# Attention beside a gated MLP mixer on one core: heads prepared in stacks of six, softmax blocks taken two at a time, gelu over two chunks, evacuations first

## The chip, the core and the metric

The kernel runs on one core of a Trainium2 chip. The metric is the time of one execution on the device in microseconds (us). Five engines work in parallel, each through its own queue in order: TensorE (PE, with its weight loads shown as PEld), VectorE (DVE), ScalarE (ACT), GpSimd (POOL) and SyncE (SP), which here only issues DMA transfers.

## The reference

The input x has 2048 tokens of 640 features. The output is x + s * g. Here s is multi-head attention with 32 heads of 20 features, and g is silu of a mixer branch; both start from the layer norm of x.

```python
x = A_x
xn = _layernorm(x)
# A: attention, H = 32, Dh = 20
q, k, v = split(xn @ wqkv)
s = softmax(q k^T * Dh**-0.5) v @ wo
# B: mixer; shift() moves four quarters of the features by +1, -1, +2, -2 tokens
h  = gelu(layernorm(xn) @ w1)
x1 = xn + shift(h) @ w2
b  = x1 + gelu(layernorm(x1) @ w3) @ w4      # w3: 640 x 1536, w4: 1536 x 640
out = x + s * silu(b)
```

## The kernel before

**A program planned by a planner.** The class `Gen` describes the work as tasks: an engine, an estimated duration, what the task reads and writes, and sometimes a due time. `Planner.schedule` carries the due times back through the dependencies to give each task a priority, plays the program forward with its own durations, and so fixes the order of each engine's queue. On the chip the queues then run in that order and wait for each other on semaphores. `strict_engines` names the engines on which a task's class comes before its due time; before, that is PE alone, where the scores and value products (class -1) precede everything else. PSUM banks are handed out by the planner from pools: two double banks for scores (`S`), three single banks (`W`) for everything else that PE computes, and one bank (`PV`) that collects the value products. A task with `rel=h` is the one that empties a bank and gives it back.

**Attention.** The 32 heads go in eight quads of four. For each quad there are four groups of 512 queries, and in each group 16 key tiles of 128 keys. For an ordinary key tile `score_act` computes the scores of two heads into a double bank, and ScalarE takes the exponential of 1024 columns at once (`exp_act`, L1239); `fnpv` (L1186) multiplies by the values and adds into `PV`. A *block* is a pair of key tiles from `BLK` of which half of the heads is taken off ScalarE. `score_both` (scores at L1197) puts two heads into a double bank for ScalarE and the other two into two `W` banks, which VectorE reads into a 16-bit integer buffer `U` (L1270). Four integer operations on `U` (L1160) then make bit patterns whose weighted sum stands for the exponential, and 16 value products (L1175) add the four variants into `PV`. `Cfg.ND` says how many blocks each of the 32 groups has, and `Cfg.order` where they stand among the key tiles. A group ends in `normalise`: VectorE copies `PV` out (L1307), the row sums go through DRAM to be spread over the partitions, inverted (L1314), sent back and broadcast (the DMA of L1318), and multiplied in (L1320). The heads then go to DRAM and from there into `OTd`, the transposed output that stays in SBUF until the end.

**Keys and queries.** `prep(q)` runs once for each quad. It projects the quad's four heads of keys and queries into four groups of 32 partitions (20 used), in 8 tiles of 20 matmuls, each emptied by VectorE (L1048, L1055). It takes the largest key of each feature (L1060), the absolute queries (L1067) and a small product to bound the scores (L1072, L1077), and writes that bound as a 21st row of the queries by four small DMAs (L1079), due `LEAD` = 20 us before the quad's first use. The columns of `wqkv` come in for each quad (L1027).

**The mixer branch.** It runs beside the attention in what PE has left over, with due times spread over the quads (`B1`, `B2`, counted in quads). `b_w12` does one chunk of 512 tokens: w1, a gelu of 2560 columns (L1502), w2 and the residual. `b_w34` does one chunk: layer norm, transposes, w3 with its columns streamed, a gelu of 6144 columns (L1555), w4 from SBUF, the residual (L1564) into `BO`, and the silu through a tanh (L1568) and a product (L1573). The gelu and the exponential are not in one table set, so each gelu brings one table load before it and one after.

**The end.** In the last quad `finish_qc` multiplies by `wo` for each group of 512 queries from `OTd`, multiplies by the gate, adds x and writes the output. `mm_tile` (its matmuls are at L740) is the helper behind every product that isn't attention.

Of the kernel before, what the change touches and what calls it, by code (L numbers as in the profile page):

```python
# [127 lines left out]
class Planner:  # L128
    def __init__(self):
# [16 lines left out]
        self.strict_engines = ("pe",)  # L146
# [124 lines left out]
    def schedule(self, verbose=False):  # L271
# [28 lines left out]
        for t in tasks:  # L300
            if t.cls and t.eng in self.strict_engines:
                t.prio = t.prio + t.cls * self.cls_penalty
# [11 lines left out]
        done = 0  # L314
# [265 lines left out]
class Cfg:  # L580
# [5 lines left out]
    def __init__(self, S=2048, D=640, H=32, F=1536):  # L586
# [13 lines left out]
        self.BLK = [(4, 5), (9, 10), (14, 15)]  # L600
        self.LAG = 3
        self.AHEAD = 3
        self.B1 = (0.4, 0.7)
        self.B2 = (3.0, 1.1)
        self.LEAD = 20000.0
        self.ND = (
            [1, 2, 3, 3],
            [3, 3, 3, 2],
            [3, 3, 3, 2],
            [3, 2, 3, 2],  # L610
            [3, 2, 3, 2],
            [3, 2, 3, 2],
# [3 lines left out]
    def order(self, quad, qc):  # L616

        nb = self.ND[quad][qc]  # L620
        used = [k for b in self.BLK[:nb] for k in b]
        ks = [k for k in range(self.NT) if k not in used]
        at = [round(j * len(ks) / nb) for j in range(nb)]
        out = []
        due = {}
        for i in range(len(ks) + 1):
            for j in range(nb):
                if due.get(j) == i or (i == len(ks) and due.get(j, 0) > i):
                    out.append(("d", j))
                    due[j] = -1  # L630
            for j in range(nb):
                if at[j] == i:
                    out.append(("b", j))
                    due[j] = i + self.LAG
            if i < len(ks):
                out.append(("k", ks[i]))
        return out
# [37 lines left out]
class Gen:  # L675
# [71 lines left out]
    def build(self, plan_only=False):  # L747
        nc, pl = self.nc, self.pl
        with contextlib.ExitStack() as es:
# [5 lines left out]
            self.do = nc.dram_tensor("heads", (2, 128, 512), BF16, kind="Internal").ap()  # L755
            self.W0 = 5
            pl.reserve = 0
# [16 lines left out]
    def program(self):  # L774
# [6 lines left out]
        self.prep_weights(0)  # L781
        self.ln1_and_transpose()
        self.prep(0)
# [4 lines left out]
        for quad in range(cfg.NQUAD):  # L788
            if quad + 1 < cfg.NQUAD:
                self.prep_weights(quad + 1)  # L790
                self.prep(quad + 1)
            if quad == 1:
                self.v_load(1)
                self.v_proj(1)
            self.run_b(quad)
            if quad == cfg.NQUAD - 1:
                self.load_wo()
            self.attn_quad(quad)
# [9 lines left out]
    def setup_consts(self):  # L808
# [26 lines left out]
          reads=[A("maskh")], writes=[A("maskh")], name="maskh")  # L835
        Mm = self.Mm = self.alloc("Mm", [2, 32], BF16)
        T("pool", 200, lambda e: e.memset(Mm[:, :, :], 0.0), writes=[A("Mm", 0), A("Mm", 1)], name="Mm0")

    def alloc_persistent(self):
# [6 lines left out]
        self.AQ = self.alloc("AQ", [S // 2], BF16)  # L846
        self.SH = self.alloc("SH", [512], BF16)
        self.MX = self.alloc("MX", [2], FP32)
        self.Wp = self.alloc("Wp", [2, KC, 92], BF16)
# [3 lines left out]
        self.NSS = 5  # L853
        self.U = self.alloc("U", [2048], U16)
        self.SS = self.alloc("SS", [self.NSS, 2048], U16)
# [5 lines left out]
        self.OTd = self.alloc("OTd", [KC, S], BF16)  # L861
        T("pool", 1500, lambda e: e.memset(self.OTd[:, KC - 1, :], 0.0), writes=[A("OTd", KC - 1, q) for q in range(4)], name="otd0")
# [12 lines left out]
        self.ssi = 0  # L875
# [144 lines left out]
    def prep_weights(self, q):  # L1020
        cfg = self.cfg
        T, A = self.T, self.A
        D, DH = cfg.D, cfg.DH
        src = self.aps["A_wqkv"].rearrange("(kc p) n -> p kc n", p=128)
        for qk in (1, 0):
            c0 = qk * D + q * cfg.QW
            T("sp", C_SP, lambda e, qk=qk, c0=c0: e.dma_start(self.Wp[:, qk, :, :], src[:, :, c0:c0 + 92]),  # L1027
              writes=[A("Wp", qk)], is_dma=True, nbytes=128 * cfg.KC * 92 * 4, name=f"ld_wp{q}_{qk}", stream=f"wp{qk}")

    def prep(self, q):  # L1030

# [4 lines left out]
        b = q % 2  # L1036
# [3 lines left out]
        for qk, dst, tag in ((1, KT, "KT"), (0, QT, "QT")):  # L1040
            for c in range(NQC):
                c0 = 512 * c
                at = [A(tag, b, c)] + ([A("QTa", b, c)] if qk == 0 else [])
                h, wa = self.mm_tile(f"{tag}{q}_{c}", KC, 512, lambda k, j, qk=qk: Wp[:, qk, k, DH * j:DH * j + 32],
                                     lambda k, j, c0=c0: xnT[:, k, c0:c0 + 512],
                                     lambda k, qk=qk, c=c: [A("Wp", qk)] + [A("xnT", k, c)], at)
                if qk == 1:
                    T("dve", c_dve(512), lambda e, h=h, c0=c0: e.tensor_scalar(KT[:, b, c0:c0 + 512], self.wbank(h)[:, 0:512],  # L1048
                                                                               mask[:, 0:1], self.eaug[:, 0:1], op0=ALU.mult, op1=ALU.add),
                      reads=[wa, A("eaug"), A("maskh")], writes=at, name=f"kev{q}_{c}", rel=h)  # L1050
                elif q == 0:
                    T("act", c_act(512) + 100, lambda e, h=h, c0=c0: e.activation(QT[:, b, c0:c0 + 512], self.wbank(h)[:, 0:512], AF.Copy, scale=mask[:, 0:1]),
                      reads=[wa, A("maskh")], writes=at, name=f"qev{q}_{c}", rel=h)
                else:
                    T("dve", c_dve(512), lambda e, h=h, c0=c0: e.tensor_scalar(QT[:, b, c0:c0 + 512], self.wbank(h)[:, 0:512],  # L1055
                                                                               mask[:, 0:1], None, op0=ALU.mult),
                      reads=[wa, A("maskh")], writes=at, name=f"qev{q}_{c}", rel=h)
        MX, Mm, AQ, SH = self.MX, self.Mm, self.AQ, self.SH
        T("dve", c_dve(cfg.S, "1x"),
          lambda e: e.tensor_reduce(MX[:, b:b + 1], KT[:, b, :], axis=AX.X, op=ALU.max, apply_absolute_value=True),  # L1060
          reads=[A("KT", b, c) for c in range(NQC)], writes=[A("MX", b)], name=f"mx{q}")
        T("dve", 210, lambda e: e.tensor_scalar(Mm[:, b, 0:4], self.maskn[:, 0:4], MX[:, b:b + 1], None, op0=ALU.mult),
          reads=[A("MX", b), A("maskn")], writes=[A("Mm", b)], name=f"mm{q}")
        h, wa = self.wtile()
        for k in range(2):
            T("dve", c_dve(cfg.S // 2, "4x"),
              lambda e, k=k: e.tensor_scalar(AQ[:, :].bitcast(U16), QT[:, b, 1024 * k:1024 * k + 1024].bitcast(U16), 0x7FFF, None, op0=ALU.bitwise_and),  # L1067
              reads=[A(t, b, c) for c in (2 * k, 2 * k + 1) for t in ("QT", "QTa")], writes=[A("AQ")], name=f"aq{q}_{k}")
            def fn(e, h=h, k=k):
                pb = self.wbank(h)  # L1070
                for c in (2 * k, 2 * k + 1):
                    ins = e.matmul(pb[32 * c:32 * c + 32, 0:512], Mm[:, b, :], AQ[:, 512 * (c % 2):512 * (c % 2) + 512], start=True, stop=True,  # L1072
                                   tile_position=(0, 32 * c))
                return ins
            T("pe", 216, fn, reads=[A("Mm", b), A("AQ")], writes=[wa] + ([A("SH")] if k == 0 else []), name=f"sh{q}_{k}",
              acq=("W", h) if k == 0 else None, tile=h.id)
        T("dve", c_dve(512), lambda e, h=h: e.tensor_scalar(SH[:, :], self.wbank(h)[:, 0:512], cfg.OFFSET / cfg.scale, None, op0=ALU.add),  # L1077
          reads=[wa], writes=[A("SH")], name=f"shev{q}", rel=h)
        T("sp", 4 * C_SP, lambda e: [e.dma_start(QT[20:128:32, b, 512 * c:512 * c + 512], SH[32 * c:32 * c + 4, :]) for c in range(NQC)],  # L1079
          reads=[A("SH")], writes=[A("QTa", b, c) for c in range(NQC)], is_dma=True, nbytes=16384, name=f"aug{q}", stream="aug", ndma=4,  # L1080
          due=self.due_quad(q) - cfg.LEAD)
# [38 lines left out]
    def attn_quad(self, quad):  # L1120
# [5 lines left out]
        KT, QT, PT, U, SS = self.KT, self.QT, self.PT, self.U, self.SS  # L1126
        VA, VP = self.VA[hf], self.VP[hf]
        PVB = self.PVB
        last = quad == cfg.NQUAD - 1
        for qc in range(NQC):  # L1130
# [8 lines left out]
            blocks = {}  # L1139
# [473 lines left out]
```

## Time and profile before

| | before |
|---|---|
| median of three executions | 956.57 us (956.25 to 956.67) |
| profiled span | 956.7 us, mean granted TensorE clock 0.985 |
| busy: ACT, PE, DVE, POOL | 887.8, 858.7, 699.7, 30.6 us |
| exponentials on ScalarE | 860 |
| block reads and bit operations on VectorE | 160 at L1270, 8 more in halves at L1273; 328 at L1160 |
| first exponential, end of the last | 43.9 us, near 941.8 us |

A line such as L1239 is a line of the kernel before. A group in the profile is all instructions of one line and form; its idle time is what its engine stood still just before them, and the arrow names the work that ended it. Busy time of PE is wide, since matmuls overlap: four of them, on four groups of columns or rows, run side by side.

### The profile page before, as it was taken

How to read it: one execution, taken by the hardware profiler on the slowest of the kernel's cores; microseconds unless marked ns; L12 is line 12 of the kernel's file. 1: busy time of each engine (PE TensorE's matmuls, PEld its weight loads, DVE VectorE, ACT ScalarE, POOL GpSimd, SP SyncE). 2: the span in 40 equal slices, each digit the busy share in tenths (PEclk: the TensorE clock that was granted, in tenths of full speed). 3: DMA queues.
4: the chain of work that ended last, by engine and by line, in shares of the span. 5: the costliest groups of instructions: out<-in, count | busy, mean ns of one | idle time of the engine just before them, and what ended most of it. 6: DMA issues, size and time to landing. Idle time of an engine off the chain costs nothing.

```text
span 956.7 us, 34900 instructions
## 1 busy us (share of the span) xinstructions
PE 858.7 (90%) x15986; PEld 379.9 (40%) x15986; DVE 699.7 (73%) x1098; ACT 887.8 (93%) x937; POOL 30.6 (3%) x59
## 2 busy tenths in 40 slices
PE   2997999899999899999999999999989879988996
PEld 2533433333433344433543444334433334423453
DVE  7647788898668788768667677686766758866756
ACT  7499999999999999999959999899998989999994
POOL 7100000000000000000000000000000000000000
PEclk9999999999999999999999999999999979999998
DMA  7110010111031111132112200221121200210223
GB/s 223 22 49 27 20 28 23 30 33 28 26 113 40 24 29 38 28 76 55 26 38 62 60 27 20 70 62 33 30 53 39 57 21 19 74 29 21 61 84 97
DMA packets 80278, 45.31 MB, mean 47 GB/s; under 512 B 55016, under 2 KB 75912, under 8 KB 80004
## 3 DMA queue, kind: packets, MB, share of 16 engines
q1 hardware_dynamic: 80132, 43.09, 16.2%
q8 instruction: 125, 2.05, 0.9%
q14 instruction: 21, 0.17, 0.1%
HBM read 32.06 MB, written 6.81 MB: 41 GB/s over the span
## 4 chain that ended last, share of the span: by engine, by line
ACT 57%; PE 30%; DVE 7%; DMA 5%; issue 1%; SPq 0%; POOL 0%; DVEq 0%
ACT arena L1239 50%; PE psum L740 11%; PE psum L1215 10%; PE psum L1186 3%; DMA arena<-recips 3%; PE psum L1197 2%; ACT arena L1555 2%; PE psum L1175 2%; DVE arena L1270 2%; ACT L1239 1%; ACT arena L1568 1%; DMA recips<-arena 1%; DVE arena L906 1%; ACT arena L1502 1%; DVE arena L1160 1%
## 5 line engine op out<-in xcount | busy, mean ns | idle before, releaser
L1239 ACT ACTIVATE arena<-psum 128x1024 bf16<-128x1024 f32 x860 | 803.9, 1037 | 36.9 <-PE psum L1197 27.5
L1215 PE MATMUL psum<-arena 128*32 128x512 bf16 x5344 | 410.6, 384 | 19.8 <-ACT arena L1239 15.3
L740 PE MATMUL psum<-arena 128*32 128x320 bf16 (+1 forms) x6224 | 377.5, 337 | 7.5 <-DVE arena L1055 1.3
L1270 DVE TENSOR_SCALAR arena<-psum 128x1024 uint16<-128x1024 f32 x160 | 195.4, 1221 | 77.4 <-PE psum L1197 76.6
L740 PEld LDWEIGHTS psum<-arena 128*32 128x32 bf16 x6224 | 161.5, 97 | 157.6 <-issue 23.9
L1160 DVE TENSOR_SCALAR arena<-arena 128x2048 uint16<-128x2048 uint16 x328 | 206.4, 688 | 1.1
L1215 PEld LDWEIGHTS psum<-arena 128*32 128x32 bf16 x5344 | 111.7, 95 | 171.7 <-ACT arena L1239 129.2
L1186 PE MATMUL psum<-arena 128*22 128x512 bf16 x1720 | 168.4, 383 | 2.4 <-ACT arena L1239 2.3
L1175 PE MATMUL psum<-arena 128*22 128x512 bf16 x1312 | 115.6, 381 | 1.7 <-DVE arena L1160 1.3
L1197 PE MATMUL psum<-arena 32*128 32x512 bf16 x712 | 76.1, 388 | 44.5 <-DVE arena L1270 20.1
L1197 PEld LDWEIGHTS psum<-arena 32*128 32x128 bf16 x712 | 19.7, 91 | 120.8 <-ACT arena L1239 67.4
L1186 PEld LDWEIGHTS psum<-arena 128*22 128x22 bf16 x1720 | 44.3, 93 | 56.7 <-issue 8.8
L1551 DVE CAST arena<-psum 128x512 bf16<-128x512 f32 x48 | 32.9, 687 | 32.5 <-PE psum L740 32.4
L1175 PEld LDWEIGHTS psum<-arena 128*22 128x22 bf16 x1312 | 33.2, 92 | 39.6 <-DVE arena L1160 6.8
L1564 DVE TENSOR_TENSOR arena<-psum,arena 128x320 bf16<-128x320 f32 x32 | 15.6, 489 | 31.3 <-PE psum L740 31.3
L1048 DVE TENSOR_SCALAR arena<-psum,arena 128x512 bf16<-128x512 f32 x32 | 25.7, 806 | 9.9 <-PE psum L740 9.6
L1320 DVE TENSOR_TENSOR arena<-arena 128x512 bf16<-128x512 f32 x31 | 21.3, 687 | 15.7 <-DMA arena<-recips 15.6
L1414 DVE SCALAR_TENSOR_TENSOR arena<-psum,arena 128x320 bf16<-128x320 f32 x32 | 15.4, 488 | 22.7 <-PE psum L740 22.6
L906 DVE BATCH_NORM_STATS2 arena<-arena 128x6 f32<-128x320 bf16 x52 | 23.3, 479 | 4.3 <-DMA arena<-in_A_x_dram 4.2
L1510 DVE TENSOR_TENSOR arena<-psum,arena 128x320 bf16<-128x320 f32 x32 | 15.6, 488 | 14.6 <-PE psum L740 14.3
L1307 DVE COPY arena<-psum 128x512 f32<-128x512 f32 x31 | 21.2, 685 | 6.7 <-PE psum L1186 5.0
L1005 PE MATMUL psum<-arena 128*32 128x128 bf16 x320 | 9.5, 291 | 17.8 <-DVE arena L920 15.0
(82 smaller groups left out, 316.9 us busy)
## 6 DMA issues: line engine op xcount, KB each, us to landing
arena<-recips SPq DMA_DIRECT2D x31, 256.0 KB
arena<-in_B_w_dram SPq DMA_DIRECT2D x48, 160.0 KB, 2.6
arena<-arena SPq DMA_DIRECT2D x124, 32.0 KB, 1.9
heads<-arena SPq DMA_DIRECT2D x28, 128.0 KB, 1.7
arena<-in_A_x_dram SPq DMA_DIRECT2D x8, 320.0 KB, 6.7
arena<-in_A_x_dram SPq DMA_DIRECT2D x16, 160.0 KB, 2.4
out_dram<-arena SPq DMA_DIRECT2D x16, 160.0 KB, 1.8
arena<-in_B_w_dram SPq DMA_DIRECT2D x1, 1920.0 KB, 9.1
```

The source lines that it names most:

```text
L740: ins = e.matmul(pb[32 * c:32 * c + 32, 0:N], lhsT(k, c), rhs(k, c), start=(k == 0), stop=(k == nk - 1), tile_position=(0, 32 * c))
L906: lambda e, li=li, n=n, hh=hh: e.bn_stats(st[:, li, 6 * hh:6 * hh + 6], xn[:, n, hD * hh:hD * hh + hD]),
L1048: T("dve", c_dve(512), lambda e, h=h, c0=c0: e.tensor_scalar(KT[:, b, c0:c0 + 512], self.wbank(h)[:, 0:512], mask[:, 0:1], self.eaug[:, 0: ...
L1160: lambda e, s=s, v=v: e.tensor_scalar(SS[:, s, :], U[:, :], 0.5, EXP_B[v], op0=ALU.mult, op1=ALU.add),
L1175: ins = e.matmul(pb[32 * i:32 * i + 22, 0:512], w, SS[:, s, at:at + 512].bitcast(BF16), start=first, stop=final, tile_position=(0, 32 * i))
L1186: ins = e.matmul(pb[32 * i:32 * i + 22, 0:512], VA[:, ql, kts[i // 2], i, :], PT[:, slots[i // 2][0].slot, 512 * (i % 2):512 * (i % 2) + 512],
L1197: return e.matmul(out, self.KT[32 * i:32 * i + 32, b, 128 * kt:128 * kt + 128], self.QT[32 * i:32 * i + 32, b, 512 * qc:512 * qc + 512], s ...
L1215: ins = e.matmul(out[32 * c:32 * c + 32, :], self.KT[:, b, 128 * kt + 32 * c:128 * kt + 32 * c + 32], self.QM[:, gb, 2 * a + jj, :], start ...
L1239: lambda e: e.activation(self.PT[:, hp.slot, :], self.psum[:, 1024 * hs.slot:1024 * hs.slot + 1024], AF.Exp, scale=cfg.scale),
L1270: return e.tensor_scalar(dst, self.psum[:, 512 * (self.W0 + lo):512 * (self.W0 + hi + 1)], a_exp, EXP_BIAS, op0=ALU.mult, op1=ALU.add)
L1320: T("dve", c_dve(512, "1x"), lambda e: e.tensor_tensor(dst, Ob[:, :], RB[:, :], op=ALU.mult), reads=[A("Ob"), A("RB")], writes=[dsta], nam ...
L1551: T("dve", c_dve(512), lambda e, h=h, fc=fc: e.tensor_copy(GT[:, fc, :], self.wbank(h)[:, 0:512]), reads=[wa], writes=at, name=f"gt_{ch}_{ ...
```

## The change

Six things are changed together.

1. *Stacks.* Only the first quad is prepared as before. The other 28 heads go in five stacks of six heads (the last has four). `stack` projects 120 dense rows of keys, then of queries, casts them into `KS`, stores them to DRAM (`dk`, `dq`), and computes the bound for six heads, which is stored as well (`ds`). `fetch` then brings a quad's four heads, rows of 2048 columns, and the bound rows into the partitions where the attention wants them. The stack is due 80 us ahead of the quad.
2. *Bits of two blocks at once.* `U` is twice as wide, and where a group has two or three blocks, the first two share their four bit operations, now 4096 columns wide. `UNITS` says where the blocks stand. `BLK` has four pairs of key tiles, and `ND` gives three blocks to more groups.
3. *Gelu over two chunks.* `b_w12` and `b_w34` take two chunks of 512 tokens, and one gelu covers both. Their due times are later accordingly.
4. *w4 streamed.* Of w4 half of the columns is in SBUF at a time; it is loaded twice for each pair of chunks. The residual goes into `xn` in place of `BO`, and the product after the tanh is one of 1280 columns in place of two of 640.
5. *O streamed.* The normalised heads go to their final rows in DRAM (`do`), and `finish_qc` loads 512 columns of them (`OTq`) when it needs them. `OTd` is gone.
6. *Evacuations first.* VectorE becomes a strict engine, and each of its tasks that gives a PSUM bank back has class -1.

The diff, cut to its core:

```diff
-        self.strict_engines = ("pe",)
+        self.strict_engines = ("pe", "dve")
...
         for t in tasks:
+            if t.eng == "dve" and t.rel is not None:
+                t.cls = -1
             if t.cls and t.eng in self.strict_engines:
                 t.prio = t.prio + t.cls * self.cls_penalty
...
-        self.BLK = [(4, 5), (9, 10), (14, 15)]
+        self.BLK = [(2, 3), (6, 7), (10, 11), (14, 15)]
...
+        self.UNITS = ((), ((3, 0, 1),), ((0, 0, 2), (2, 1, 2)), ((0, 0, 2), (2, 1, 2), (6, 0, 1)),
+                      ((0, 0, 2), (1, 1, 2), (4, 0, 2), (5, 1, 2)))
+        self.HPS = 6
...
-        self.LEAD = 20000.0
+        self.LEAD = 80000
         self.ND = (
             [1, 2, 3, 3],
-            [3, 3, 3, 2],
-            [3, 3, 3, 2],
-            [3, 2, 3, 2],
-            [3, 2, 3, 2],
-            [3, 2, 3, 2],
+            [3, 3, 3, 3],
+            [3, 3, 3, 3],
+            [3, 3, 3, 3],
+            [3, 3, 3, 3],
+            [3, 3, 3, 3],
             [3, 3, 3, 3],
             [3, 3, 2, 1])
...
         for quad in range(cfg.NQUAD):
+            while self.stacks < 5 and (4 + cfg.HPS * self.stacks) // 4 <= quad + 1:
+                self.stack(self.stacks)
+                self.stacks += 1
             if quad + 1 < cfg.NQUAD:
-                self.prep_weights(quad + 1)
-                self.prep(quad + 1)
+                self.fetch(quad + 1)
...
-        self.U = self.alloc("U", [2048], U16)
-        self.SS = self.alloc("SS", [self.NSS, 2048], U16)
+        self.U = self.alloc("U", [4096], U16)
+        self.SS = self.alloc("SS", [4, 4096], U16)
...
-        self.OTd = self.alloc("OTd", [KC, S], BF16)
-        T("pool", 1500, lambda e: e.memset(self.OTd[:, KC - 1, :], 0.0), writes=[A("OTd", KC - 1, q) for q in range(4)], name="otd0")
...
+        T("pool", 1500, lambda e: e.memset(self.KT[:, 1, :], 0.0), writes=[A("KT0")], name="kt0")
+        T("pool", 1500, lambda e: e.memset(self.QT[:, 1, :], 0.0), writes=[A("QT0")], name="qt0")
...
+    def stack(self, st):
...
+        due = self.due_quad(h0 // 4) - cfg.LEAD
...
+            T("sp", C_SP, lambda e, dst=dst: e.dma_start(dst[DH * h0:DH * (h0 + nh), :], KS[0:DH * nh, :]), reads=ksa,
+              writes=[("dkq", qk, st)], is_dma=True, nbytes=120 * 4096, name=f"dk{qk}_{st}", stream=f"dk{qk}", due=due)
...
+    def fetch(self, quad):
...
+                return [e.dma_start(dst[32 * i:32 * i + DH, b, :], src[DH * (4 * quad + i):DH * (4 * quad + i + 1), :]) for i in range(4)]
...
+    def block_bits(self, quad, qc, blocks, ends):
...
+        w = 2048 * len(blocks)
...
+            T("dve", c_dve(w, "4x"), lambda e, v=v, dst=dst: e.tensor_scalar(dst, U[:, 0:w], 0.5, EXP_B[v], op0=ALU.mult, op1=ALU.add),
+              reads=halves, writes=dsta, name=f"s{quad}_{qc}_{blocks[0][0]}_{v}", due=cfg.T0 + (self.nact + cfg.LAG) * cfg.STEP)
...
-        T("sp", C_SP, lambda e: e.dma_start(do[ob], self.On[:, ob, :]), reads=[A("On", ob)], writes=[("do", ob)], is_dma=True,
-          nbytes=128 * 1024, name=f"o0{quad}_{qc}", stream="o0")
...
+            return [e.dma_start(do[r0 + DH * i:r0 + DH * i + DH, 512 * qc:512 * qc + 512], self.On[32 * i:32 * i + DH, ob, :]) for i in range(4)]
...
-        T("act", 2600 + c_act(KC * 512), lambda e: e.activation(hx[:, i, :, :], hx[:, i, :, :], AF.Gelu_apprx_tanh),
-          reads=at, writes=at, name=f"gelu1_{ch}", due=self.due_quad(cfg.B1[0] + cfg.B1[1] * ch))
+        T("act", 2600 + c_act(2 * KC * 512), lambda e: e.activation(hx[:, :, :, :], hx[:, :, :, :], AF.Gelu_apprx_tanh),
+          reads=at, writes=at, name=f"gelu1_{c0}", due=self.due_quad(cfg.B1[0] + cfg.B1[1] * (c0 + 1)))
...
+            T("sp", C_SP, lambda e, hs=hs: e.dma_start(W4[:, :, :], w4src[:, :, hs]),
+              writes=[A("W4")], is_dma=True, nbytes=FC * 128 * D, name=f"ld_w4_{c0}_{hh}", stream="w4")
```

## The prediction

> **What bounds the kernel now.** I read the busy totals first, then the chain of waits, then what ScalarE's groups wait for, then windows cut along the kernel's eight quads. The totals and the chain on the page:
>
> ```profile
> PE 858.7 (90%) x15986; PEld 379.9 (40%) x15986; DVE 699.7 (73%) x1098; ACT 887.8 (93%) x937; POOL 30.6 (3%) x59
> ...
> ACT 57%; PE 30%; DVE 7%; DMA 5%; issue 1%; SPq 0%; POOL 0%; DVEq 0%
> ```
>
> ScalarE is busiest and carries most of the chain. PE's 90% is not a rate of work, so I counted its passes (below). Then the groups, ScalarE's and VectorE's: line, engine, operation, shapes and count, then busy us and mean ns of one, then the idle time before them and what ended it.
>
> ```profile
> L1239 ACT ACTIVATE arena<-psum 128x1024 bf16<-128x1024 f32 x860 | 803.9, 1037 | 36.9 <-PE psum L1197 27.5 <-PE psum L1215 7.7 <-PE psum L1186 0.4
> L1555 ACT ACTIVATE arena<-arena 128x6144 bf16<-128x6144 bf16 x4 | 21.3, 5324 | 0.0
> L1239 ACT ACT_TABLE_LOAD x8 | 10.3, 1283 | 0.1
> L1568 ACT ACTIVATE arena<-arena 128x1280 bf16<-128x1280 bf16 x8 | 10.1, 1267 | 5.0 <-DVE arena L1564 5.0
> L1502 ACT ACTIVATE arena<-arena 128x2560 bf16<-128x2560 bf16 x4 | 9.3, 2337 | 0.0
> ```
>
> ```profile
> L1160 DVE TENSOR_SCALAR arena<-arena 128x2048 uint16<-128x2048 uint16 x328 | 206.4, 688 | 1.1
> L1270 DVE TENSOR_SCALAR arena<-psum 128x1024 uint16<-128x1024 f32 x160 | 195.4, 1221 | 77.4 <-PE psum L1197 76.6
> ```
>
> An exponential (L1239) costs 803.9/860 = 0.935 us of ScalarE. The eight table loads of L1239 are the way back from each of the eight gelus (L1502, L1555); eight more of 1283 ns stand before the gelus themselves. L1160 are the bit operations of the blocks, L1270 their reads of PSUM. Last, windows (PE, weight loads, DVE, ACT, POOL busy, the clock, DMA) over the body and the tail, and over three quads:
>
> ```profile
> 57.00:941.80 884.80, 814.23 (x14966) 354.08 (x14962) 649.21 (x966) 850.02 (x879) 7.93 (x15) 0.99 0.16 42
> 941.80:957.00 15.20, 6.91 (x156) 3.80 (x148) 11.97 (x28) 0.85 (x1) 0.00 (x0) 0.80 0.37 118
> 258.00:364.00 106.00, 98.22 (x1768) 40.16 (x1756) 83.84 (x132) 105.48 (x112) 1.11 (x2) 0.98 0.17 50
> 472.00:578.00 106.00, 99.99 (x1976) 46.49 (x1972) 76.80 (x122) 94.36 (x96) 1.02 (x1) 1.00 0.19 46
> 686.00:796.00 110.00, 96.26 (x1692) 40.54 (x1688) 72.45 (x100) 101.94 (x103) 0.00 (x0) 0.94 0.16 41
> ```
>
> The first exponential starts at 43.9 us. From 43.9 to 57 ScalarE was busy 12.96 of 13 us. From there to 941.8 it idles 34.8 us (884.8 - 850.0). So 956.7 is about 43.9 before the exponentials, 863 of ScalarE work, 34.8 idle, 15.2 of tail. Where nothing interferes (258 to 364) ScalarE is full; the idle time gathers in two quads, 11.6 us and 8.1 us. What ends it, from the table of waits (us in total, times, longest):
>
> ```profile
> PEld psum L1197 <- DVE arena L1270: 35.1, 35, 2.6
> ...
> ACT arena L1239 <- PE psum L1197: 27.5, 19, 7.5
> ...
> DVE arena L1320 <- DMA arena<-recips: 15.6, 14, 2.6
> ```
>
> ScalarE waits for the block scores of L1197 (7.5 of the 27.5 is the start), and those wait for VectorE to empty PSUM banks at L1270.
>
> **What the Trainium skill says.** "ScalarE: Activation LUTs", What ACT_TABLE_LOAD costs, prices a switch at 1283 ns of load and a drain of about 1380 ns. The trace agrees on 1283, but shows no gap around the load (idle 0.1 us), so I use the load alone. "VectorE: DVE Perf Modes", the section on the errata, says that SBUF operations pay a fixed cost per instruction, once for a large tile. The 2048-wide row of L1160 fits: 206.4/328 = 0.629 us, of which 2048/4/0.96 = 533 ns is streaming, at the four elements a cycle and 0.96 GHz that the page gives, and 96 ns fixed. "Trainium Kernel Development and Optimization", Performance Expectations, warns that matmul busy time misleads because matmuls are pipelined; here too, 90% busy stands beside an 80% count of passes. "DMA: Bandwidth & Descriptors", Latency, speaks of about 2 us of fixed cost to HBM; the trace's small transfers through DRAM land in 1.4 to 1.8 us.
>
> **The change, part by part.**
>
> *Exponentials.* A block of two key tiles takes two 1024-wide exponentials off ScalarE. The table ND sums to 82 before (1024 - 2x82 = 860, as counted) and to 90 after, so 844. Saved: 16 x 0.935 = 15.0 us of ScalarE, on the path.
>
> *Gelu over two chunks.* Four gelus for eight: 8 table loads fewer, 8 x 1.283 = 10.3 us, and four fixed costs fewer. From 5.324 us for 6144 and 2.337 us for 2560 columns, the slope is 0.833 ns and the fixed part 0.20 us, so 0.8 us. Saved: 11.1 us of ScalarE. The price is one piece of about 10.4 + 2.6 us in which no exponential runs; PE has the stacks and the other products to do meanwhile.
>
> *VectorE work of the blocks.* Eight blocks more are 16 PSUM reads of 1.22 us (19.5). The bit operations become 120 of 4096 columns (28 groups with three blocks and 2 with two give 30 pairs, x 4, estimated at 1.067 + 0.096 = 1.16 us) and 120 of 2048 (28 third blocks and 2 lone ones, x 4, 0.629): 139.6 + 75.5 = 215.1 against 206.4. Added: 28.2 us.
>
> *Stacks.* Seven per-quad preparations go. Each costs VectorE 4 x 0.81 + 4 x 0.75 + 2.28 + 0.21 + 2 x 0.42 + 0.69 = 10.3 us by their rows. Five stacks come, each 8 casts of 0.69 and the same rest, 9.5 us. Net 72 - 48 = 24 us less VectorE. So VectorE stays at about 704 us, some 76% of the new span: not the bound.
>
> *PE.* A pass is four column-tiled matmuls side by side; 8 matmuls of 512 columns take 0.43 us in the chain, so 0.215 us a pass. A pair of key tiles costs 8 score and 2 value passes, a block 2 score, 1 value and 4 bit passes: 8 blocks save 24 passes. Two preparations fewer (280 - 200) save 80. Together 104 x 0.215 = 22 us. The passes of before come to 2932 of 512 columns and 896 of 320 (0.137 us each, 2.44/18 from a long run): 753 us, and 20480 columns of transposes, 40 times 0.215 = 9 us, make 762, or 80% of the span. After: 740. PE is eased by as much as ScalarE, and stays under it.
>
> *Transfers.* A stack goes out in 4 KB rows and comes back as four sets of rows per quad, plus the shifts. The chain is three dependent landings, at 2 to 5 us each by the trace, and the due time lies 80 us ahead of the quad's first use, so I cost it at nothing: it hides behind the exponentials of the quad before. What it puts at risk is SyncE's queue, which is in order: behind a waiting store stand the four small transfers of the softmax sums, and behind those VectorE's multiply at L1320. Bounds: 0, or 15.6 us more of that wait. I take 0, since the seven shift transfers that go waited in the same way. Storing the heads into their final rows replaces a double hop; half-width w4 comes four times at 960 KB, at most the 9.1 us that the 1920 KB took, with other PE work in front.
>
> *Evacuations first.* On VectorE every task that frees a PSUM bank now precedes the bit operations, the sums and the normalising. This aims at the 35.1 us of L1197 on L1270. Behind a waiting evacuation stand the bit operations, whose readers (L1175) now have four key tiles, about 7.5 us of exponentials, before the group ends. Bounds: it removes between 0 and some 20 us of ScalarE's 34.8 us idle. I take 6.
>
> *Start and tail.* POOL gets two 128x2048 memsets (2.1 us by L862's row) and a few selects in place of one, and is full between 7.5 and 13 us where its power operation carries the chain: 0 to 2.6 us later, taken as 1. The tail keeps its chain, 15.2 us.
>
> Sum: 956.6 - 15.0 - 11.1 - 6 + 1 = 925.5, say 926 us.
>
> **The rivals.** *Less work, but lumps:* the second pair of chunks is due later. Its sixteen w4 tiles, 192 passes of 0.137 = 26 us of PE, run from quad 6.6 to 7.3, into the output projections of quad 7 (another 26 us or so), and the silu waits on them as in the 11.6 us quad. If idle grows by 15 us instead of falling by 6, 946. For: 472 to 578 shows how one such lump costs ten. Against: GT is double-buffered, and blocks relieve PE in exactly those quads. *Slower:* a stall at each of seven quad boundaries, on SyncE's order or a late fetch, of 5 us (one broadcast landing), plus the lumps: 926 + 35 + 5 = 966. For: VectorE already waits on DMA at L1320. Against: 80 us of lead. *Idle nearly gone:* the stalls at L1197 come from PE and banks both, and both ease; with 12 us idle left, 926 - 17 = 909. For: 258 to 364 with 0.5 us idle. Against: B work still comes in lumps.
>
> **How the numbers follow.** Forecast 0.60, lumps 0.15, idle nearly gone 0.14, slower 0.09, and 0.02 for about no change. Faster by over 0.2% holds the forecast, the lumps and the third: 0.89. The bounds (ScalarE's saving of 26 us is firm, idle between 14 and 58) give 907 to 950, which leaves out the slower case and the edges of the others.
>
> **What would show it.** Right: 844 exponentials, 8 ScalarE table loads fewer, ScalarE near 862 us, VectorE near 704, L1197's wait on L1270 under 25 us though there are more blocks, idle before the exponentials under 37. Wrong: exponentials that wait for fetched keys or queries at quad boundaries, longer waits at the sums' DMAs, VectorE waiting on PE in front of ready bit operations until the next group's value products stall, or output projections left over after the last exponential.

## The result and the profile after

The changed kernel takes 930.48 us (928.66 to 931.26), the kernel before 956.45 us: ratio 0.9726, 95% interval 0.9709 to 0.9743. All figures are of fast executions: one of the four of the kernel before with 90 blocks alone took 1460 us at a granted clock of 0.56 and is left out, so its median is 985.58 us and not the 987 that a later expectation names.

The lines that follow are from the page of the changed kernel and answer to the first of before. In it L1320 is the exponential, L1296 the ordinary scores, L1239 the ordinary value products, L1278 the block scores, L1270 the block value products, L1352 the block reads, L1259 the bit operations, L1402 the multiplication by the sums, L1630 the long gelu, L1646 the silu. In runs with another text these lines stand a few lines higher or lower.

```profile
PE 838.2 (90%) x15562; PEld 365.0 (39%) x15562; DVE 708.9 (76%) x991; ACT 861.4 (93%) x909; POOL 35.0 (4%) x68
...
ACT 65%; PE 25%; DMA 5%; DVE 4%; issue 1%; SPq 0%; DVEq 0%
```

ScalarE lost 26.4 us of work and carries more of the chain than before. Its groups and VectorE's block groups:

```profile
L1320 ACT ACTIVATE arena<-psum 128x1024 bf16<-128x1024 f32 x844 | 788.9, 1034 | 36.6 <-PE psum L1278 24.3 <-PE psum L1239 7.1 <-PE psum L1296 4.7
L1630 ACT ACTIVATE arena<-arena 128x12288 bf16<-128x12288 bf16 x2 | 20.9, 10446 | 0.0
L1646 ACT ACTIVATE arena<-arena 128x1280 bf16<-128x1280 bf16 x8 | 10.1, 1266 | 0.0
L1577 ACT ACTIVATE arena<-arena 128x5120 bf16<-128x5120 bf16 x2 | 8.9, 4471 | 0.0
...
L1320 ACT ACT_TABLE_LOAD x4 | 5.1, 1283 | 0.1
```

```profile
L1352 DVE TENSOR_SCALAR arena<-psum 128x1024 uint16<-128x1024 f32 x178 | 217.5, 1222 | 97.5 <-PE psum L1278 96.1
L1259 DVE TENSOR_SCALAR arena<-arena 128x4096 uint16<-128x4096 uint16 x120 | 141.2, 1219 | 0.2
L1259 DVE TENSOR_SCALAR arena<-arena 128x2048 uint16<-128x2048 uint16 x120 | 77.2, 689 | 1.7 <-PE psum L1270 1.3
```

There are 844 exponentials at an unchanged 0.935 us, four gelus with half of the table loads, and no wait left before the silu (L1646; 5.0 us before). In the table of waits the bank wait of the block scores has shrunk from 35.1 to 12.3 us, though there are more blocks, and the wait for the broadcast of the sums from 15.6 to 7.2 (this last one turns out below to be no fixed gain):

```profile
ACT arena L1320 <- PE psum L1278: 24.3, 20, 7.2
...
PEld psum L1278 <- DVE arena L1352: 12.3, 17, 1.3
...
DVE arena L1402 <- DMA arena<-recips: 7.2, 7, 2.5
```

To say where the time went I cut each trace at the start of its first and the end of its last exponential. The last exponential of before starts at 941.6 us and ends at 942.6, not near 941.8 as the table and the prediction have it, so its tail is 14.1 us and not 15.2. Windows of the changed kernel, body and tail, and then of the body of the kernel before (columns as before: length, then PE, weight loads, DVE, ACT, POOL busy, the clock, DMA):

```profile
45.26:912.30 867.04, 803.50 (x14694) 343.75 (x14690) 661.25 (x872) 837.42 (x864) 11.59 (x24) 0.99 0.20 55
912.30:929.50 17.20, 9.06 (x228) 5.62 (x220) 13.96 (x32) 0.01 (x1) 0.00 (x0) 0.82 0.30 96
```

```profile
43.92:942.60 898.68, 826.92 (x15178) 359.16 (x15178) 657.59 (x980) 863.86 (x892) 9.65 (x19) 0.99 0.16 42
```

The cut gives a ledger that the experiments use too (us, from the traces; ScalarE and idle are within the body):

| kernel | start | ScalarE | idle | tail | span |
|---|---|---|---|---|---|
| before | 43.9 | 863.9 | 34.8 | 14.1 | 956.7 |
| changed | 45.3 | 837.4 | 29.6 | 17.2 | 929.5 |
| difference | +1.4 | -26.5 | -5.2 | +3.1 | -27.2 |

So the gain is ScalarE's work, almost to the microsecond, and the rest nearly cancels. This agrees with the prediction term by term except for the tail, but it doesn't show that each part is worth what its term says. That is what the experiments were for.

### The profile page after: what moved, and what is told of

Same layout as the page of the kernel before. It is cut to its first block, busy times and chain, and to the rows that moved or that the text cites. A ratio compares the mean times of both kernels' runs of the same rounds, so it can differ in the third digit from the quotient of the medians.

```text
span 929.5 us, 34050 instructions
## 1 busy us (share of the span) xinstructions
PE 838.2 (90%) x15562; PEld 365.0 (39%) x15562; DVE 708.9 (76%) x991; ACT 861.4 (93%) x909; POOL 35.0 (4%) x68
## 4 chain that ended last, share of the span: by engine, by line
ACT 65%; PE 25%; DMA 5%; DVE 4%; issue 1%; SPq 0%; DVEq 0%
ACT arena L1320 60%; PE psum L740 11%; PE psum L1296 7%; PE psum L1239 3%; PE psum L1278 2%; ACT arena L1630 2%; DMA arena<-recips 2%; DMA arena<-in_B_w_dram 1%; PE psum L1270 1%; DMA recips<-arena 1%; ACT arena L1577 1%; DVE arena L918 1%; DVE arena L1352 1%; DMA arena<-in_A_x_dram 1%; ACT L1320 1%
## 5 line engine op out<-in xcount | busy, mean ns | idle before, releaser
L1320 ACT ACTIVATE arena<-psum 128x1024 bf16<-128x1024 f32 x844 | 788.9, 1034 | 36.6 <-PE psum L1278 24.3
L1296 PE MATMUL psum<-arena 128*32 128x512 bf16 x5088 | 390.3, 384 | 28.2 <-ACT arena L1320 22.6
L740 PE MATMUL psum<-arena 128*32 128x320 bf16 (+1 forms) x5904 | 350.6, 335 | 15.2 <-ACT arena L1630 9.1
L1352 DVE TENSOR_SCALAR arena<-psum 128x1024 uint16<-128x1024 f32 x178 | 217.5, 1222 | 97.5 <-PE psum L1278 96.1
L1259 DVE TENSOR_SCALAR arena<-arena 128x2048 uint16<-128x2048 uint16 (+1 forms) x240 | 218.3, 954 | 1.9 <-PE psum L1270 1.3
L740 PEld LDWEIGHTS psum<-arena 128*32 128x32 bf16 x5904 | 151.3, 98 | 154.6 <-issue 25.0
L1296 PEld LDWEIGHTS psum<-arena 128*32 128x32 bf16 x5088 | 105.4, 95 | 181.7 <-ACT arena L1320 147.2
L1239 PE MATMUL psum<-arena 128*22 128x512 bf16 x1688 | 164.1, 381 | 5.6 <-DVE arena L1389 2.8
L1270 PE MATMUL psum<-arena 128*22 128x512 bf16 x1440 | 117.1, 380 | 5.0 <-DVE arena L1259 5.0
L1278 PE MATMUL psum<-arena 32*128 32x512 bf16 x776 | 81.6, 386 | 13.1 <-DVE arena L1352 5.1
L1239 PEld LDWEIGHTS psum<-arena 128*22 128x22 bf16 x1688 | 43.2, 93 | 57.3 <-ACT arena L1320 7.6
L1278 PEld LDWEIGHTS psum<-arena 32*128 32x128 bf16 x776 | 21.0, 91 | 89.7 <-ACT arena L1320 55.9
L1270 PEld LDWEIGHTS psum<-arena 128*22 128x22 bf16 x1440 | 34.3, 92 | 47.3 <-DVE arena L1259 9.4
L1626 DVE CAST arena<-psum 128x512 bf16<-128x512 f32 x48 | 32.9, 686 | 12.3 <-PE psum L740 12.2
L1641 DVE TENSOR_TENSOR arena<-psum,arena 128x320 bf16<-128x320 f32 x32 | 15.6, 488 | 28.7 <-PE psum L740 28.5
L1124 DVE CAST arena<-psum 128x512 bf16<-128x512 f32 x40 | 27.5, 688 | 11.1 <-PE psum L740 10.4
L1402 DVE TENSOR_TENSOR arena<-arena 128x512 bf16<-128x512 f32 x31 | 21.3, 686 | 7.2 <-DMA arena<-recips 7.2
L918 DVE BATCH_NORM_STATS2 arena<-arena 128x6 f32<-128x320 bf16 x52 | 23.3, 480 | 3.5 <-DMA arena<-in_A_x_dram 3.4
L1185 DVE CAST arena<-psum 128x320 bf16<-128x320 f32 x32 | 15.3, 487 | 9.7 <-PE psum L740 9.7
```

The lines of the kernel that those rows point to most:

```text
L740: ins = e.matmul(pb[32 * c:32 * c + 32, 0:N], lhsT(k, c), rhs(k, c), start=(k == 0), stop=(k == nk - 1), tile_position=(0, 32 * c))
L918: lambda e, li=li, n=n, hh=hh: e.bn_stats(st[:, li, 6 * hh:6 * hh + 6], xn[:, n, hD * hh:hD * hh + hD]),
L1124: T("dve", c_dve(512), lambda e, h=h, c=c: e.tensor_copy(KS[:, 512 * c:512 * c + 512], self.wbank(h)[:, 0:512]), reads=[wa], writes=[A("KS ...
L1239: ins = e.matmul(pb[32 * i:32 * i + 22, 0:512], VA[:, ql, kts[i // 2], i, :], PT[:, slots[i // 2][0].slot, 512 * (i % 2):512 * (i % 2) + 512],
L1259: T("dve", c_dve(w, "4x"), lambda e, v=v, dst=dst: e.tensor_scalar(dst, U[:, 0:w], 0.5, EXP_B[v], op0=ALU.mult, op1=ALU.add), reads=halves ...
L1270: ins = e.matmul(pb[32 * i:32 * i + 22, 0:512], wv, dst[:, at:at + 512].bitcast(BF16), start=first, stop=final, tile_position=(0, 32 * i))
```

## The experiments

Each run is compared by its ratio to the kernel before, run beside it on the same chip.

**Undoing one part at a time.** First the order of VectorE's queue:

```diff
-        self.strict_engines = ("pe", "dve")
+        self.strict_engines = ("pe",)
...
-            if t.eng == "dve" and t.rel is not None:
-                t.cls = -1
```

> The changed kernel with VectorE's queue ordered by due time alone, as before the change. My theory (evacuations first removes waits of the block scores for banks, some 6 us of ScalarE's idle time): 936 us, idle before the exponentials 6 us longer. Rival 1 (the order is worth nothing, the idle time fell because PE was relieved): 929 to 932. Rival 2 (the order carries much of the gain, since more blocks need the banks): 942 or more.

Measured: 960.99 us, ratio 1.0034 (1.0018 to 1.0051). Without this one part, and with the constants as they are, the change gains nothing. By its number the second rival came true, at five times what I had put on the part. Its reason did not: the block scores wait for VectorE's reads 27.9 us, less than the 35.1 of the kernel before. The windows of this run, body and tail, show both places of the loss:

```profile
45.19:931.80 886.61, 801.59 (x14370) 338.81 (x14366) 652.80 (x852) 839.92 (x864) 12.65 (x24) 0.97 0.19 51
931.80:961.50 29.70, 20.92 (x552) 13.95 (x544) 22.28 (x51) 0.00 (x1) 0.00 (x0) 0.92 0.52 160
```

Idle time is 886.6 - 839.9 = 46.7 us (29.6 in the changed kernel), and the tail 29.7 (17.2): 552 matmuls, 536 of them in products outside the attention, are left when the exponentials are over, against 228. The mixer branch fell behind: the last silu starts at 905.6 us here and at 835.0 in the changed kernel, and much of what needs its result is pushed past the end. PE also did little during the long gelu. Windows over the two pieces of 13 us (two table loads and the gelu of 12288 columns), changed kernel first, then this run:

```profile
530.10:543.20 13.10, 9.46 (x200) 4.67 (x204) 12.90 (x19) 13.04 (x5) 0.00 (x0) 0.92 0.15 38
751.30:764.30 13.00, 4.24 (x64) 1.56 (x68) 4.01 (x5) 12.97 (x3) 0.00 (x0) 0.68 0.07 24
```

```profile
578.50:591.60 13.10, 1.52 (x52) 0.82 (x44) 1.45 (x3) 13.04 (x5) 0.00 (x0) 0.74 0.24 66
819.30:832.40 13.10, 5.18 (x64) 1.47 (x68) 5.86 (x7) 13.04 (x5) 0.00 (x0) 0.67 0.09 27
```

PE stands still for 11.6 and 8 us here, and for 3.6 and 9 in the changed kernel. What ends the longest stand is told by the tables of waits, first that of this run from 500 to 600 us (where L1276 is the block scores and L1318 the exponential), then that of the changed kernel:

```profile
PE psum L1276 <- ACT arena L1318: 12.7, 1, 12.7
```

```profile
PE psum L740 <- ACT arena L1630: 9.1, 2, 7.7
```

In the second pieces PE ends up at the mixer's next product, which needs that very gelu: 7.7 us of wait in the changed kernel, 5.6 here. The first piece of this run is another case. Block scores stand at the head of PE's queue and wait 12.7 us for an exponential that stands behind the gelu, and everything behind them waits too.

Next the count of blocks, with the rest of the change kept:

```diff
-            [3, 3, 3, 3],
-            [3, 3, 3, 3],
-            [3, 3, 3, 3],
-            [3, 3, 3, 3],
-            [3, 3, 3, 3],
-            [3, 3, 3, 3],
+            [3, 3, 3, 2],
+            [3, 3, 3, 2],
+            [3, 2, 3, 2],
+            [3, 2, 3, 2],
+            [3, 2, 3, 2],
+            [3, 3, 3, 3],
```

> The changed kernel with the 82 blocks of the table ND of before in place of 90. My theory (ScalarE's work sets the time, 16 exponentials of 0.935 us): 945 us, ScalarE 15 us busier. Rival (VectorE and PE stand in the way as much, and blocks load VectorE with 3.5 us each): VectorE loses 28 us, idle time of ScalarE shrinks with it, and the time is 938 or less.

Measured: 950.06 us, ratio 0.992 (0.990 to 0.994), 19 us above the changed kernel at equal footing (0.992 - 0.9726 of 957 us). ScalarE's body rose by 16.3 us to 853.7 and idle time from 29.6 to 33.3. At these constants the rival falls: fewer blocks, though VectorE is 36 us less busy (673.0), leave no less idle time.

The gelus one chunk at a time:

```diff
-        T("act", 2600 + c_act(2 * KC * 512), lambda e: e.activation(hx[:, :, :, :], hx[:, :, :, :], AF.Gelu_apprx_tanh),
+        for i in range(2):
+            T("act", 2600 + c_act(KC * 512), lambda e, i=i: e.activation(hx[:, i, :, :], hx[:, i, :, :], AF.Gelu_apprx_tanh),
...
-        T("act", 2600 + c_act(2 * FC * 512), lambda e: e.activation(GT[:, :, :, :], GT[:, :, :, :], AF.Gelu_apprx_tanh),
+            T("act", 2600 + c_act(FC * 512), lambda e, i=i: e.activation(GT[:, i, :, :], GT[:, i, :, :], AF.Gelu_apprx_tanh),
...
```

The gelu of the first chunk of each pair also gets a due time one chunk earlier.

> The changed kernel with one gelu for each chunk of 512 tokens (eight in all), everything else kept. My theory: 8 table loads and 4 fixed costs come back, 11.1 us of ScalarE, 941.5 us. Rival (the long gelu piece costs idle time around it, so batching is worth less than its loads): 936 or less.

Measured: 949.87 us, ratio 0.9927 (0.9906 to 0.9949): 12.2 us of ScalarE's body (849.6; 11.1 expected), and 6.9 us of idle time on top (36.5), which I had not expected.

The bits of one block at a time, which also moves the second block to a later place in its group:

```diff
-        self.UNITS = ((), ((3, 0, 1),), ((0, 0, 2), (2, 1, 2)), ((0, 0, 2), (2, 1, 2), (6, 0, 1)),
+        self.UNITS = ((), ((3, 0, 1),), ((0, 0, 1), (4, 0, 1)), ((0, 0, 1), (3, 0, 1), (6, 0, 1)),
```

> The changed kernel with the bit operations for one block at a time (2048 columns, 360 of them), the blocks spread evenly over the group. My theory (VectorE isn't the bound): VectorE about 11.7 us busier (120 pairs of 0.629 for 120 of 1.16), time up by 4 us at most. Rival (VectorE is close to the bound, or pairs are what makes 90 blocks possible): 938 or more.

Measured: 951.88 us, ratio 0.9935 (0.9913 to 0.9956). VectorE is 11.1 us busier (720.0), as computed, but idle time grew by 22.8 us to 52.4 (in an execution of 955.3 us, 3.4 above the median), and by its number the rival is the one that fits. A later run shows that pairs aren't needed for 90 blocks. ScalarE's waits in that run:

```profile
ACT arena L1320 <- PE psum L1278: 27.6, 24, 7.2
ACT arena L1320 <- PE psum L1239: 17.7, 5, 5.5
ACT arena L1320 <- PE psum L1296: 9.3, 13, 1.5
```

The second line is new in size (7.1 us in the changed kernel). I read it as scores that stand behind value products; which of the two edits, single bits or other places, brings it was not run apart.

By now three single undoings cost some 20 us each and one 30. Their sum, 87 us, is over three times the gain, so the parts are not terms of a sum. Two more runs measured parts by themselves.

**One part alone in the kernel before.** The new table ND alone (the reverse of the ND diff, with the block places of before):

> The kernel before with the new table ND alone: 90 blocks. My theory (ScalarE sets the time, VectorE has room): 956.5 - 15 = 941.5 us. Rival (the stacks are what makes room: with per-quad preparation VectorE rises by some 37 us to 737 us and the bank waits grow): idle time takes back half or more of it, 949 or more.

Measured: 985.58 us, ratio 1.0287 (1.0262 to 1.0312): some 27 us slower, where my theory had 15 faster. ScalarE has its 13.4 us less to do, and idles 78.3 us in place of 34.8. Its waits name the places:

```profile
ACT arena L1239 <- PE psum L1197: 30.5, 22, 7.5
ACT arena L1568 <- DVE arena L1564: 19.5, 4, 9.6
ACT arena L1239 <- PE psum L1215: 17.8, 20, 2.5
ACT arena L1239 <- PE psum L1186: 16.3, 5, 6.2
```

L1568 is the silu: it stands in ScalarE's queue where the plan expected its input, up to 9.6 us too early, and every exponential behind it waits.

Evacuations first alone, the reverse of the first diff:

> The kernel before with evacuations first on VectorE as its only change. My theory: 6 us of idle time go, 950.5 us. Rival 1 (worth nothing): within 2 us of 956.5. Rival 2 (the order alone takes most of the 34.8 us of idle time): 940 or less.

Measured: 954.45 us, ratio 0.995 (0.9936 to 0.9963), 4 to 5 us faster. The profiled execution, the fastest of 16, idles 28.4 us, 6.4 less than the one of before, which was slower than its median by 2; so the 4 to 5 us are the better figure, close to the 6 of the prediction. The bank wait of the block scores fell further, from 35.1 to 22.4: most of it was not on ScalarE's path. The same part is worth 4 us here and 30 us there.

**A change that should do nothing.** The date at which the stacks are due:

```diff
-        self.LEAD = 80000
+        self.LEAD = 60000
```

> The changed kernel with the stacks due 60 us ahead of their quad and not 80. Nothing waits for a stack by my theory, so the time changes only by what any other order of the same tasks changes: within 3 us of 930.5, and this is the size below which I read nothing into one edit. Rival (the stacks come just in time): longer by 5 us or more, with scores waiting for fetched rows.

Measured: 930.09 us, ratio 0.9705 (0.9681 to 0.973). The stacks come in good time: the trace shows no engine waiting for fetched keys or queries. This edit makes a new plan as well, so not every new plan costs 20 us.

**The tail.** In the changed kernel's tail the reciprocal of the last group stands behind evacuations: the transpose of the sums starts at 913.1 us, the reciprocal at 918.1. This run puts the last group's chain ahead:

```diff
-              writes=[("PV", 0), A("Ob")], name="pv_tr")
+              writes=[("PV", 0), A("Ob")], name="pv_tr", cls=-2)
```

and the same for the three operations after it.

> The changed kernel with the last group's four normalising operations on VectorE (transpose, reciprocal, product, transpose) ahead of all evacuations. My theory (in the tail, eight evacuations of the output projection are put ahead of the reciprocal, 5 us on the path that sets the end): 926.5 us, 4 us less. Rival (the tail is set by the projections left over on PE): within 1 us of 930.5.

Measured: 931.11 us, ratio 0.9723 (0.9697 to 0.9749). The reciprocal came at 914.3 and the last transpose at 915.9 (919.8), and the tail stayed at 17.2 us. By its number the rival holds: the order within the tail is of no account. What fills the tail is not PE alone, which is busy 8.9 of the 17.2 us; VectorE, with the evacuations and what follows them, is busy 13.8.

**The constants.** What undoing a part may also undo is the fit of the plan. The due times of the mixer (B1, B2), T0, STEP and LAG decide where in the in-order queues the gelus, the silus and their products stand; the change took them over unchanged from the kernel before. The last runs therefore give each version constants of its own: those of the candidates for which the planner's plan came out shortest by its own durations. Evacuations not first, with such constants:

```diff
-        self.T0 = 45000.0
-        self.STEP = 960.0
+        self.T0 = 45821.83636491798
+        self.STEP = 918.4980612560263
...
-        self.LAG = 3
+        self.LAG = 4
...
-        self.B1 = (0.4, 0.7)
-        self.B2 = (3.0, 1.1)
+        self.B1 = (0.37, 0.6)
+        self.B2 = (3.18, 1.04)
```

> The changed kernel with VectorE's queue in order of due time alone, as in the earlier run at 961 us, but with the due-time constants (B1, B2, T0, STEP, LAG) chosen anew for that order. My theory now (the 30 us belong to how well the constants fit the order in which PE's mixer work can get its banks, and not to evacuations first as such): 932 to 938 us, the last silu back at 840 us or earlier. Rival (evacuations first is needed once there are 90 blocks, whatever the constants): 950 or more.

Measured: 934.53 us, ratio 0.9749 (0.9723 to 0.9774). Of the 30 us, some 27 came back from five constants. The last silu starts at 856.6 us, later than I had put it, but the tail is back at 17.8 and idle time at 30.3. The bank wait of the block scores is 29.1 us, as large as in the run at 961 (27.9), so the 27 us were not that wait. In the changed kernel evacuations first isn't needed for 90 blocks. What is needed is a plan that fits.

The kernel before with its constants alone chosen anew (B1 = (0.46, 0.71), B2 = (3.39, 1.06), T0 = 42115.9, STEP = 951.7):

> The kernel before with nothing changed but the due-time constants (B1, B2, T0, STEP). ScalarE's work stays at 888 us. My theory (part of the 34.8 us of idle time is the fit of the constants): 944 to 950 us. Rival (the constants of before fitted it well): within 2 us of 956.5.

Measured: 949.29 us, ratio 0.9896 (0.9874 to 0.9918). ScalarE's work is unchanged; idle time fell from 34.8 to 23.3 us, though the bank wait of the block scores is still 27.8 (35.1 before), and the silu no longer waits (5.0 before). So some 10 of the 34.8 us of idle time that I had read as waits for banks were the fit of the constants.

The kernel before with 90 blocks, evacuations first and fitted constants (B1 = (0.49, 0.7), B2 = (3.27, 1.04), T0 = 46111.5, STEP = 936.9), and none of the other parts:

> The kernel before with 90 blocks, evacuations first and due-time constants chosen anew; no stacks, bits of one block at a time, eight gelus, w4 and the heads in SBUF. My theory (16 exponentials fewer are worth 15 us as soon as the constants fit): 932 to 938 us. Rival (the stacks and the paired bits are what makes room for 90 blocks): 950 or more, as 90 blocks alone took 987.

Measured: 930.33 us, ratio 0.9704 (0.968 to 0.9728): as fast as the whole change. Its windows, body and tail:

```profile
44.10:915.10 871.00, 818.66 (x15106) 356.29 (x15102) 696.97 (x1029) 849.14 (x876) 9.97 (x19) 1.00 0.16 44
915.10:929.80 14.70, 5.16 (x109) 2.47 (x100) 11.27 (x27) 0.06 (x1) 0.00 (x0) 0.72 0.35 113
```

ScalarE has 11.7 us more to do than in the changed kernel (the gelus are single), idle time is 21.9 against 29.6, the tail 14.7 against 17.2. VectorE is at 739.2 us, 80% of the span, and still not the bound. No silu waits any more (19.5 us with 90 blocks alone). These are the 90 blocks that took 985.58 us a few runs ago; evacuations first and the constants came together here, so this run doesn't tell their shares.

**The version that beats both.** The changed kernel with fitted constants (B1 = (0.5, 0.7), B2 = (2.56, 1.22), STEP = 946.4), and the two memsets of POOL behind the transposes of the start:

```diff
-        T("pool", 1500, lambda e: e.memset(self.KT[:, 1, :], 0.0), writes=[A("KT0")], name="kt0")
-        T("pool", 1500, lambda e: e.memset(self.QT[:, 1, :], 0.0), writes=[A("QT0")], name="qt0")
...
+        late = [A("xnT", self.cfg.KC - 1, 3)]
+        T("pool", 1500, lambda e: e.memset(self.KT[:, 1, :], 0.0), reads=late, writes=[A("KT0")], name="kt0")
+        T("pool", 1500, lambda e: e.memset(self.QT[:, 1, :], 0.0), reads=late, writes=[A("QT0")], name="qt0")
```

> The changed kernel with due-time constants chosen anew (B1, B2, STEP), and with the two memsets of POOL put behind the layer norm's transposes. The start should come 1 to 1.4 us earlier and the idle time and tail shrink by some 5 us: 923 to 926. Rival (the constants of the change are already as good as any): 929 to 931.

Measured: 923.11 us, ratio 0.9627 (0.960 to 0.9654). Body and tail:

```profile
43.30:903.70 860.40, 806.15 (x14682) 343.47 (x14678) 660.74 (x871) 836.40 (x864) 18.29 (x24) 0.99 0.21 56
903.70:921.40 17.70, 9.82 (x241) 6.01 (x236) 13.97 (x32) 0.00 (x0) 0.00 (x0) 0.81 0.30 94
```

The start is 2.0 us earlier (43.3), idle time 5.6 us less (24.0), the tail about as it was. The ledger with the runs (us; each row is one execution, up to 3.4 us from the median of its kernel):

| kernel | ScalarE | idle | tail | ratio to before |
|---|---|---|---|---|
| before | 863.9 | 34.8 | 14.1 | 1 |
| evacuations first alone | 862.9 | 28.4 | 14.6 | 0.995 |
| 90 blocks alone | 850.5 | 78.3 | 14.1 | 1.0287 |
| constants alone | 864.8 | 23.3 | 16.3 | 0.9896 |
| 90 blocks, evacuations first, constants | 849.1 | 21.9 | 14.7 | 0.9704 |
| changed | 837.4 | 29.6 | 17.2 | 0.9726 |
| changed, evacuations not first | 839.9 | 46.7 | 29.7 | 1.0034 |
| the same with constants | 838.5 | 30.3 | 17.8 | 0.9749 |
| changed, constants and start | 836.4 | 24.0 | 17.7 | 0.9627 |

## Why the prediction was right, and where it wasn't

*The bound and the exponentials.* Right. 844 exponentials at the old price, and in every run of the ledger ScalarE's own work is within some 3 us of what was computed. What the ledger adds is that the work doesn't become time unless idle time holds still: 16 exponentials fewer came out as some 27 us more, and, in a plan that fits them, as a gain.

*Gelu over two chunks.* The 11.1 us of work are right (12.2 in the run that undoes it). The step "PE has the stacks and the other products to do meanwhile" held for the first piece, where PE worked 9.5 of 13 us, and failed for the second, 4.2 of 13, where the mixer's next product waits for the same gelu. Length alone is not the cause: in the kernel before PE worked 7.3, 7.4, 6.7 and 1.2 us in its four pieces of 8 us. With fitted constants the version with single gelus and without the other parts stands at 930.3 beside 923.1, so stacks, paired bits, paired gelus and the streams together came out at about 7 us: 12.7 us less work on ScalarE and a start 0.8 earlier, against 2.1 more idle time and 3.0 more tail. Each set of constants is only the best of a limited choice, and the second run also has its memsets moved, so this is no exact price.

*VectorE and the stacks.* 708.9 us against 704 forecast: the wide bit operation takes 141.2/120 = 1.18 us (1.16 estimated), and VectorE is not the bound, not even at 80%. PE was eased as counted (15562 matmuls, 424 fewer; the 104 passes of the forecast are 416). That stacks or pairs are what makes room for more blocks, the rival of two runs, is refuted by the kernel before that takes 90 blocks in 930 us without either.

*Transfers.* Costed at nothing, and for the stacks they were: bringing their due date 20 us closer didn't matter. That the wait at the broadcast fell from 15.6 to 7.2 us is no property of the change: with most of its parts kept it is 14.6 us in the fastest version, 26.6 with single bits and 31.2 with 82 blocks, the upper bound of the prediction. How much of the idle time of those last two comes from it is not known.

*Evacuations first.* Taken at 6 us, and the idle time did fall by 5.2, although the wait that the part aims at fell by 22.8. As the worth of this part the number holds in the kernel before (4 to 5 us by the medians). In the changed kernel it depends on the constants: with those taken over from before, the part decides between 930 and 961; with constants fitted on both sides it is 923.1 against 934.5, where idle time differs by 6.3 us and the moved memsets account for about 2. The step that failed is the one that treated the parts as terms of a sum.

*Start and tail.* The start came 1.4 us later (1 forecast), from the memsets: with them moved back it is 2.0 us earlier, while new constants alone moved the start by 0.2 at most. The tail was forecast unchanged and grew by 3.1 us, most of what the sum missed. It is the rival of the lumps in small: the output projections left over after the last exponential, named there as a sign, are 45 passes in a row on PE.

*Slips in the working.* The bounds of 907 to 950 do not come out of the idle range given for them: with 26 us saved and the later start, 14 to 58 us of idle time give some 911 to 955. A pass of 320 columns is 2.44/18 = 0.136 us, not 0.137. Neither changes the forecast.

So the total was right by ScalarE's arithmetic and by the luck that idle time stayed near its old value. What stays open: the undoing of pairs, of paired gelus and of the added blocks costs 4 to 23 us of idle time and was not run with fitted constants, so how much of it belongs to those parts is not known. Nor is it known which of the constants matter most.

## What to carry to other kernels

In a kernel whose queues are ordered by a planner, count the bound engine's work to forecast a change, and forecast its idle time as a range that the plan decides: here it ran from 22 to 78 us at nearly the same work. Before a part is called good or bad, give the version with it and the version without it due times of their own; undoing it under constants that happen to suit it measures the misfit too. During a long instruction on the bound engine the others work on only if their queues hold, at the head, something that needs neither its result nor a buffer that it keeps from coming free.

## What the runs showed of the hardware

The clock granted to TensorE fell where PE ran out of work during a gelu: 0.68 in the piece at 751 us and 0.92 in the one at 530, 0.74 and 0.67 in the run with evacuations not first, against 0.99 over the body (0.97 in that run). The pause is paid for again when PE comes back. In the changed kernel the eight matmuls of an ordinary score took 0.61 us at the start of the first piece, twice over 1 us after it, and 0.60 again from 548 us on:

```profile
530.16 0.61 PE L1296 MATMUL psum<-arena 128*32 128x512 bf16 x8
...
544.26 1.04 PE L1296 MATMUL psum<-arena 128*32 128x512 bf16 x8 [0.28 <-ACT arena L1320]
...
546.04 1.07 PE L1296 MATMUL psum<-arena 128*32 128x512 bf16 x8
```

Over the 9.8 us after this piece the clock is 0.76 and ScalarE idles 1.4 us; over the 9.7 us after the second it is 0.89 and ScalarE idles 0.2.

Each table load between exponentials and gelus took 1283 ns, with next to no idle time around it (0.1 us in all before the four of L1320). The exponential's price stayed at 0.935 us in both kernels.
